# Another written order for the 700 pieces of a kernel's first phase

## The chip, the cores and the metric

The kernel runs on one core of one Trainium2 chip. The metric is the device time of one execution in microseconds. The kernel before took 900.28 us, the median of three runs (898.86, 900.65, 900.28).

## What is computed

Eight batches of 8 heads, 576 tokens, 64 channels. Attention has two parts that are added: one over queries, keys and values averaged in groups of four tokens and repeated four times, and one over a band of 7 tokens. The 4608 x 512 result goes through two weight matrices with a gate between them.

```python
q_d, k_d, v_d = (a.reshape(B, H, S // 4, 4, D).mean(axis=3) for a in (q, k, v))
out_up = np.repeat(sm_attn(q_d, k_d, v_d), 4, axis=2)
scores = np.where(np.abs(pos[:, None] - pos[None, :]) < 4, scale * q @ k.T, -1e9)
out_local = softmax(scores) @ v
x = (out_up + out_local)            # as 4608 x 512
h = x @ w_in                        # 512 x 2048
g = np.where(h >= 1, h, np.where(h <= -1, 0.0, (h + 1) ** 2 / 4))
out = g @ w_out                     # 2048 x 512
```

## The kernel before

Two heads make a pair; 32 pairs, four for each batch. Tokens go through the weight matrices in chunks: one of 512, eight of 384, and two of 512 at the end. The hidden 2048 columns are 16 blocks, f = 0 to 15. Each operand of a large product is split into two words, a high one and the difference to it (`xh`/`xl`, the two halves of a weight block, `gh`/`gl`), and each product takes three matmuls, here called a triple: high by high, high by low, low by high.

The kernel has a first phase, up to the end of the first chunk, and a second phase with a loop over the other chunks. The second phase is not changed. In it the scheduler of the framework places the instructions. The first phase is written as a table, `ORDER`: 700 words that stand for pieces of work. Each piece issues the instructions of one function, in the order of the table, and each engine (TensorE is PE, VectorE is DVE, ScalarE is ACT, GpSimd is POOL, and SP issues the loads) runs its own in that order and waits at the head of its queue. What stands ahead of the table (identity, band, casts of both) is set among the first pieces by the scheduler.

The words: `4.sl@hi1` is pair 4's local scores into the PSUM pool hi1. `lq`, `lk`, `lv`, `lp` load; `qd` and `kd` sum groups of four tokens; `sl` and `sp` are scores, local and pooled; `mx`, `ms`, `ex`, `su`, `nl` and `mp`, `mq`, `e0` to `e2`, `np` are the parts of the two softmaxes; `tl` and `tp` transpose, `al` and `ap` copy that out of PSUM; `pl` and `pp` are the products with the values; `xd`, `x`, `xh`, `xl` write the pair's part of x in two words. `8.lq` to `8.lp` load for pair 8, which belongs to the second phase. `i3.ld` loads block 3 of w_in (512 KB) and `o3.ld` of w_out, `c1` to `c6` unpack it: c1 and c2 on ACT (c2 of odd w_out blocks on DVE), c3 and c4 on DVE, c5 on ACT, c6 on POOL, which writes the low half. `f2.s0` to `f2.s3` are the four triples of the first product for block 2, `u1`, `sq`, `u2`, `gh`, `gl` its gate (DVE, ACT, DVE, ACT, POOL), `m2.0` to `m2.3` its triples of the second product into the four output banks o0 to o3. `f16.s0` to `f16.s3` are already block 0 of the second chunk.

Lines of note: L311 is the band matmul of the local scores, whose left operand is `ident_r` (cast on ACT in L178); L323 the local scores; L377 the pooled scores; L803 is c1, L812 c2, L816 c3, L819 c4, L822 c5 and L826 c6; L847 is a triple's matmul of the first product and L902 of the second; L884 is gl; L910 copies a bank of results and L912 stores it; L643 is the first matmul of pair 8 in the second phase, in the function `join`.

Of the kernel before, what the change touches and what calls it, by code (L numbers as in the profile page):

```python
# [89 lines left out]


ORDER = """
    0.lq 0.z 0.lk 1.lq 1.z 1.lk 0.qd 2.lq 2.z 0.kd 0.sl@hi1 0.sp@hi0 2.lk 1.qd 0.mx 0.mp 0.ms 3.lq
# [4 lines left out]
    1.al i0.c3 i1.ld 0.tp 3.ep 0.vd 2.mq 3.rc 2.e1 1.pp@lo0 3.np 2.e2 3.nl 2.e0 o1.ld 0.ap 2.ep
    3.tl@hi1 2.rc o0.c1 2.nl 3.vs@lo1 3.al o0.c3 3.tp o0.c2 2.np 4.lq 2.tl@hi1 i1.c1 o0.c4 2.vs@hi0
    2.al i2.ld i1.c3 1.pl i1.c2 2.tp o1.c1 i1.c4 0.pp@hi1 1.xh o2.ld o1.c3 2.vd 4.qd 2.ap 1.xl 0.pl  # L100
    1.yh 3.ap o1.c2 2.pp@hi0 i3.ld 3.vd 1.yl 0.xh o1.c4 i2.c1 0.xl 3.pp@lo1 0.yh i2.c3 i0.c2 4.lv
    0.yl o1.c5 i0.c4 4.sl@hi1 o2.c1 o1.c6 o3.ld i2.c2 3.pl 4.mx 2.pl i0.c5 i2.c4 3.xh 4.ms i0.c6
    4.lp 2.xh 3.yh 3.xl i2.c5 4.sp@hi1 i4.ld 2.yh 2.xl f0.s0 4.ex i2.c6 3.yl 4.mp f0.s1 o0.c5 2.yl
    i3.c1 4.su f0.s2 o0.c6 o4.ld i1.c5 f0.s3 4.mq 4.vd o3.c1 i1.c6 4.e1 f0.u1 4.e0 5.lq o2.c3 f1.s0
    4.e2 i3.c3 f0.sq f1.s1 4.ep o3.c3 5.lk o2.c2 f0.u2 f1.s2 i3.c2 4.rc f1.s3 o2.c4 i5.ld f0.gh
    f2.s0 4.nl i4.c1 f0.gl f2.s1 f1.u1 o4.c1 f2.s2 5.qd o5.ld o2.c5 f2.s3 i3.c4 f1.sq m0.0 4.np
    o2.c6 i3.c5 f1.u2 m0.1 i6.ld f2.u1 f1.gh i3.c6 4.tp@hi1 5.kd i5.c1 m0.2 o3.c2 4.ap f1.gl m0.3
    f2.sq o6.ld f3.s0 o5.c1 f2.u2 4.tl@hi1 i5.c3 f2.gh f3.s1 o3.c4 4.al f3.s2 5.lp i4.c3 i5.c2
    o4.c3 f3.s3 o5.c3 o3.c5 i7.ld 4.pl@hi1 i5.c4 i4.c2 4.pp o5.c2 o3.c6 i6.c1 m1.0 4.xd o4.c2 m1.1
    5.lv i4.c4 o6.c1 4.x f2.gl m1.2 i4.c5 5.vd i8.ld m1.3 4.xh 5.sl@hi1 i4.c6 i5.c5 f3.u1 i7.c1  # L110
    m2.0 5.mx i5.c6 6.lk m2.1 f3.sq 5.ms f4.s0 4.xl 6.lq f3.u2 5.ex f4.s1 f3.gh f4.s2 i9.ld i6.c3
    i8.c1 f4.s3 o4.c4 i6.c2 m2.2 o6.c3 f4.u1 i7.c3 o4.c5 f5.s0 o8.ld f4.sq i6.c4 o6.c2 f5.s1 f4.u2
    o5.c4 i6.c5 m2.3 o6.c4 i7.c2 5.sp@hi1 f4.gh o4.c6 o7.ld f5.s2 f5.s3 f5.u1 o6.c5 5.su f5.sq
    f3.gl i6.c6 o5.c5 6.qd i9.c1 f5.u2 i10.ld o6.c6 o8.c1 f6.s0 6.kd f6.s1 5.mp f6.s2 o9.ld 5.mq
    o7.c1 f6.s3 f4.gl m3.0 5.e0 f6.u1 5.e2 m3.1 i7.c4 5.e1 6.lp m3.2 i8.c3 i10.c1 5.ep o5.c6 m3.3
    5.rc o10.ld i7.c5 5.nl m4.0 f6.sq 5.np i7.c6 f5.gh m4.1 f6.u2 o9.c1 m4.2 i11.ld o7.c3 i8.c2
    m4.3 o8.c3 o7.c2 f5.gl f7.s0 o8.c2 f7.s1 f6.gh o11.ld i10.c3 f7.s2 o10.c1 o7.c4 f7.s3 i10.c2
    i9.c3 5.tp@hi1 o8.c4 i9.c2 i12.ld 5.ap i10.c4 m5.0 o8.c5 i9.c4 m5.1 i8.c4 i10.c5 m5.2 f6.gl
    i9.c5 o13.ld m5.3 i8.c5 5.tl@hi1 f7.u1 o11.c1 i9.c6 m6.0 f7.sq m6.1 o12.ld o7.c5 o10.c3 m6.2
    i12.c1 f7.u2 i8.c6 m6.3 5.al f9.s0 o9.c3 f7.gh i13.ld i12.c3 o10.c2 f8.s0 o9.c2 o7.c6 f8.s1  # L120
    i11.c1 f8.s2 i12.c2 o10.c4 i15.ld f8.s3 o13.c1 o9.c4 5.pl@hi1 i11.c3 o12.c1 5.pp 5.xd 5.x f8.u1
    o8.c6 o10.c5 6.lv 6.vd f9.s1 o9.c5 f7.gl f9.s2 f8.sq i14.ld i11.c2 f9.s3 f8.u2 i10.c6 6.sl@hi1
    5.xh f9.u1 i13.c1 m7.0 o13.c3 7.lp f9.sq 6.mx o10.c6 m7.1 i15.c1 o13.c2 m7.2 7.lq 6.ms o9.c6
    f8.gh m7.3 f9.u2 7.lk 6.ex f10.s0 5.xl i14.c1 6.sp@hi1 o14.ld f10.s1 f9.gh 6.mp f8.gl f10.s2
    6.su f10.s3 7.qd f9.gl o15.ld m8.0 6.mq f10.u1 6.e1 m8.1 6.e0 7.kd m8.2 f10.sq i11.c4 6.e2 m9.0
    i12.c4 i11.c5 m9.1 6.ep f10.u2 o14.c1 i11.c6 m9.2 6.rc i12.c5 6.nl m8.3 f10.gh i12.c6 6.np
    f11.s0 o15.c1 f11.s1 o11.c3 f12.s0 o13.c4 f11.s2 o11.c2 f10.gl o13.c5 f11.s3 o12.c3 f12.s1
    o11.c4 o12.c2 m10.0 f11.u1 o13.c6 o11.c5 6.tp@hi1 f11.sq f12.s2 i13.c3 6.ap f12.s3 f11.u2
    o11.c6 i13.c2 m9.3 f11.gh o12.c4 6.tl@hi1 f12.u1 f11.gl m10.1 o12.c5 6.al m10.2 f12.sq i14.c3
    m10.3 i13.c4 i14.c2 6.pl@hi1 f12.u2 o12.c6 i13.c5 6.pp 7.lv 7.vd 8.lp f12.gh m11.0 i13.c6 6.xd  # L130
    m11.1 6.x m11.2 i14.c4 6.xh m11.3 o14.c3 i14.c5 i15.c3 7.sl@hi1 8.lq 8.lk o14.c2 o15.c3 f12.gl
    i15.c2 o15.c2 f13.s0 7.mx f13.s1 i14.c6 7.ms m12.0 m12.1 7.ex i15.c4 f14.s0 o14.c4 i15.c5
    f14.s1 o15.c4 o14.c5 f13.s2 6.xl o15.c5 f13.s3 m12.2 f13.u1 i15.c6 7.sp@hi1 f13.sq f14.s2 7.mp
# [1125 lines left out]
```

## Time and profile before

| | |
|---|---|
| median of the runs | 900.28 us |
| profiled execution, first to last instruction | 900.0 us |
| PE busy | 885.3 us |
| DVE, ACT, POOL busy | 563.7, 467.9, 375.0 us |
| first phase (to the last triple of f16) | 155.85 us |
| mean granted TensorE clock | 0.997 |

The profiled execution's own time stands in the profile only as this span; it is 0.3 us below the median of the runs. A busy PE is not PE at its peak, since matmuls overlap: the pitch from one start to the next says more than the duration. PE's clock has two levels, 1.2 and 2.4 GHz; a granted clock of 1.0 is the upper one.

### The profile page before, as it was taken

What the parts mean: (1) busy time and instruction counts of PE and PEld (TensorE: products, weight loads), DVE (VectorE), ACT (ScalarE), POOL (GpSimd) and SP (SyncE); (2) the same over time, 40 slices, a digit from 0 to 9 for tenths busy, and PEclk for the clock granted to TensorE, in tenths of its full rate; (3) what the DMA queues carried; (4) which work ended last, traced back from release to release, by engine and by line L of the source; (5) the groups of instructions that cost most, each with busy time, mean ns of one, the idle gap of its engine ahead of it and who ended that gap; (6) DMA issues with size and microseconds to landing.
All of it is one profiled execution on the core that took longest, in us unless ns stands there. A gap on an engine that the chain in (4) does not pass through costs nothing.

```text
span 900.0 us, 19773 instructions
## 1 busy us (share of the span) xinstructions
PE 885.3 (98%) x7808; PEld 798.0 (89%) x7808; DVE 563.7 (63%) x1077; ACT 467.9 (52%) x1025; POOL 375.0 (42%) x361
## 2 busy tenths in 40 slices
...
GB/s 344 120 213 319 126 57 53 97 110 128 90 115 115 91 106 116 122 120 116 113 103 89 101 133 103 105 139 92 91 127 106 83 51 83 122 109 141 105 126 53
DMA packets 67884, 106.47 MB, mean 118 GB/s; under 512 B 5808, under 2 KB 33456, under 8 KB 67792
## 3 DMA queue, kind: packets, MB, share of 16 engines
...
q8 instruction: 61, 1.00, 0.4%
...
q10 hardware_dynamic: 144, 0.05, 0.0%
...
## 4 chain that ended last, share of the span: by engine, by line
PE 84%; DVE 7%; ACT 4%; issue 3%; POOL 2%; DMA 0%; SPq 0%; DVEq 0%; ACTq 0%; POOLq 0%
PE ffn_o L902 37%; PE ffn_h L847 28%; PE ffn_h L1015 7%; PE score_ps L643 2%; PE turn_ps L771 1%; PE value_ps L667 1%; DVE m L819 1%; PE local_ps L768 1%; PE value_ps L625 1%; DVE m L816 1%; DVE u L869 1%; DVE u L875 1%; POOL gl L884 1%; ACT u L872 1%; DVE sums L924 1%
## 5 line engine op out<-in xcount | busy, mean ns | idle before, releaser
L884 POOL TENSOR_TENSOR gl<-u,gh 128x384 fp32r<-128x384 f32 (+1 forms) x176 | 197.0, 1120 | 400.4 <-ACT gh L881 320.3
L902 PE MATMUL ffn_o<-w_o,gh 128*128 128x512 f32 x1152 | 347.5, 383 | 0.0
L847 PE MATMUL ffn_h<-xh,w_i 128*128 128x384 f32 (+1 forms) x1184 | 301.2, 336 | 2.5 <-POOL w_i L826 2.1
L902 PEld LDWEIGHTS ffn_o<-w_o,gh 128*128 128x128 f32 x1152 | 212.0, 190 | 25.2 <-issue 0.6
L847 PEld LDWEIGHTS ffn_h<-xh,w_i 128*128 128x128 f32 x1184 | 209.5, 189 | 16.9 <-POOL w_i L826 2.9
L902 PE MATMUL ffn_o<-w_o,gl 128*128 128x512 f32 x576 | 218.9, 380 | 0.4 <-POOL gl L884 0.4
L847 PE MATMUL ffn_h<-xl,w_i 128*128 128x384 f32 (+1 forms) x592 | 197.3, 333 | 0.0
L872 ACT ACTIVATE u<-u 128x384 f32<-128x384 f32 (+1 forms) x176 | 97.4, 553 | 133.5 <-DVE u L869 133.5
L881 ACT CAST gh<-u 128x384 fp32r<-128x384 f32 (+1 forms) x176 | 95.3, 542 | 118.8 <-DVE u L875 117.3
L869 DVE TENSOR_SCALAR u<-m 128x384 f32<-128x384 f32 (+1 forms) x160 | 76.1, 476 | 127.3 <-ACT m L868 126.9
L875 DVE SCALAR_TENSOR_TENSOR u<-m,u 128x384 f32<-128x384 f32 (+1 forms) x160 | 103.2, 645 | 78.0 <-ACT u L872 78.0
L902 PEld LDWEIGHTS ffn_o<-w_o,gl 128*128 128x128 f32 x576 | 109.3, 190 | 16.4 <-POOL gl L884 0.8
L847 PEld LDWEIGHTS ffn_h<-xl,w_i 128*128 128x128 f32 x592 | 111.9, 189 | 2.2
L868 ACT COPY m<-ffn_h 128x384 f32<-128x384 f32 (+1 forms) x132 | 63.8, 484 | 51.1 <-PE ffn_h L847 42.4
L720 ACT ACTIVATE sl<-sl 128x640 f32<-128x640 f32 x24 | 17.7, 739 | 55.1 <-POOL sl L694 55.1
L581 POOL TENSOR_TENSOR xl<-x,xh 128x576 fp32r<-128x576 f32 (+4 forms) x32 | 35.3, 1110 | 16.6 <-ACT xh L580 16.6
L826 POOL TENSOR_TENSOR w_o<-m,w_o 128x512 fp32r<-128x512 f32 x16 | 24.1, 1517 | 31.2 <-ACT w_o L822 31.2
L924 DVE SCALAR_TENSOR_TENSOR sums<-sums 128x128 f32<-128x128 f32 (+1 forms) x72 | 33.0, 459 | 1.6
L694 POOL TENSOR_TENSOR sl<-sl,mxl 128x640 f32<-128x640 f32 x24 | 30.2, 1260 | 2.3 <-DVE mxl L693 1.7
L924 DVE SCALAR_TENSOR_TENSOR words<-sums,words 128x512 fp32r<-128x512 f32 x16 | 17.7, 1109 | 17.7 <-ACT words L928 17.7
L826 POOL TENSOR_TENSOR w_i<-m,w_i 128x512 fp32r<-128x512 f32 x16 | 22.6, 1415 | 11.6 <-ACT w_i L822 11.4
L1041 POOL TENSOR_TENSOR m<-both 128x256 f32<-128x256 f32 x14 | 10.7, 765 | 39.0 <-DVE both L1040 33.8
(179 smaller groups left out, 1183.4 us busy)
## 6 DMA issues: line engine op xcount, KB each, us to landing
...
```

The source lines that it names most:

```text
L581: nc.gpsimd.tensor_tensor(xl[:, p, dst], x[:, part], xh[:, p, dst], op=ALU.subtract)
L826: nc.gpsimd.tensor_tensor(w[:, 1], raw[name, f, "m"], w[:, 0], op=ALU.subtract)
L847: ins = nc.tensor.matmul(htiles[c, f], wi[:, wt, cc * P : (cc + 1) * P], turns(xt[:, cc, ts]), start=(cc == 0 and xt is xh and wt == 0), s ...
L868: utiles["copied"] = nc.scalar.copy(m, h)
L869: nc.vector.tensor_scalar(utiles[c, f], m if c > 0 else h, -1.0, 1.0, op0=ALU.max, op1=ALU.add)
L872: nc.scalar.activation(u, u, AF.Square, scale=0.5)
L875: utiles["last"] = nc.vector.scalar_tensor_tensor(u, utiles["m"] if c > 0 else h, 1.0, u, op0=ALU.max, op1=ALU.min)
L881: nc.scalar.copy(gh, utiles[c, f])
L884: nc.gpsimd.tensor_tensor(gl, utiles.pop((c, f)), gh, op=ALU.subtract)
L902: ins = nc.tensor.matmul(o, gt[:, ts], turns(weights["o", f][:, wt, :]), start=f == 0 and n == 0, stop=f == NFC - 1 and n == 2,)
L924: return nc.vector.scalar_tensor_tensor(out, a, 1.0, b, op0=ALU.mult, op1=op)
L1015: ins = nc.tensor.matmul(ps, left(wt, k), right(xt, k), start=not more and k == 0 and wt == xt, stop=k == 1 and xt == 1, skip_group_check= ...
```

## The change

The table is replaced by another with 704 words. They are the same pieces, and four new ones, `r.0` to `r.3`: the copy of an output bank and its store, which `m15.0` to `m15.3` did before as their last act. Loads, unpacking, attention and products all stand in another order; the second product takes the four banks in another order from block to block. Three functions now make their PSUM tile whichever piece of the two that share it comes first, and three calls of `keep_up` (extra matmuls, of which both tables ask for none) are gone.

```diff
 ORDER = """
-    0.lq 0.z 0.lk 1.lq 1.z 1.lk 0.qd 2.lq 2.z 0.kd 0.sl@hi1 0.sp@hi0 2.lk 1.qd 0.mx 0.mp 0.ms 3.lq
...
-    8.lv 7.pp m13.3 7.xd 7.x m15.0 m15.1 7.xh m14.3 7.xl m15.2 m15.3 f16.s3
+    0.lq 0.lk 0.z 1.lq 0.sl@hi1 1.lk 0.qd 0.kd i1.ld i1.c1 0.sp@hi0 0.mx 0.mp o3.ld 2.lq 0.mq 2.lk
...
+    f13.gl f15.s2 f14.s3 7.e2 f12.gl f15.s3 7.ep 7.rc o13.c5 7.nl f14.u1 o14.c6 7.np f15.u1 f14.sq
+    m12.2 o15.c5 o13.c6 f15.sq m12.0 f14.u2 m11.1 f14.gh m12.1 f16.s0 f15.u2 m13.2 7.tp@hi1 6.xl
+    m13.0 m12.3 m13.3 o15.c6 7.ap f15.gh f14.gl f15.gl 7.tl@hi1 m14.0 7.vd m15.0 7.al f16.s1
+    7.pl@hi1 7.pp@hi1 7.xd m13.1 m14.3 m14.1 7.x f16.s2 m14.2 7.xh 7.xl m15.3 m15.1 m15.2 r.0 r.1
+    8.lv r.2 8.lk f16.s3 r.3 8.lp
 """.split()
...
         def vs(pool, tag, spare=0):
-            ps = t["tp_ps"] = pool.tile([P, 2, 512], F32, name="tp_ps", tag=tag)
-            keep_up(ps[:, 1, 384:], spare)
+            if "tp_ps" not in t:
+                t["tp_ps"] = pool.tile([P, 2, 512], F32, name="tp_ps", tag=tag)
+            ps = t["tp_ps"]
...
         elif piece == 2:
             raw["low", name, f] = t[:, :, 0]
-            if (name, f, "m") in raw and (name, f) not in ON_VECTOR:
+            if (name, f) not in ON_VECTOR:
                 raw["low", name, f] = t.rearrange("p n t -> p (n t)")[:, 0:512]
...
-        if f == NFC - 1:
-            osb = temp("osb")
-            nc.scalar.copy(osb, o)
-            rows = out[CHUNKS[c][0] : CHUNKS[c][0] + CHUNKS[c][1], :].rearrange("(a b) d -> b a d", a=2)
-            nc.sync.dma_start(rows[t * P // 2 : (t + 1) * P // 2], osb)
+        if f == NFC - 1 and c > 0:
+            result(c, t)
+
+    def result(c, t):
+
+        osb = temp("osb")
+        nc.scalar.copy(osb, places["o"](t))
+        rows = out[CHUNKS[c][0] : CHUNKS[c][0] + CHUNKS[c][1], :].rearrange("(a b) d -> b a d", a=2)
+        nc.sync.dma_start(rows[t * P // 2 : (t + 1) * P // 2], osb)
...
+            elif kind == "r":
+                result(0, int(what))
```

The first place is ACT's queue at the very start. Before, from the load of `members` on:

```order
L239 DMA own_2_87<-members 128x360
L180 ACT_TABLE_LOAD
L180 CAST band_r<-band_sb 128x64
L178 CAST ident_r<-ident 128x128
L394 ACTIVATE sp,sums<-sp_ps,mxp 128x144 x2
L363 ACTIVATE sl<-sl_ps 128x640
```

And now, the same stretch:

```order
L240 DMA own_2_87<-members 128x360
L181 ACT_TABLE_LOAD
L181 CAST band_r<-band_sb 128x64
L803 ACTIVATE raw_i_150<-raw_i_150 128x512
L179 CAST ident_r<-ident 128x128
L395 ACTIVATE sp,sums<-sp_ps,mxp 128x144
L812 ACTIVATE raw_i_150<-raw_i_150 128x512
```

The first piece of block 1 of w_in (L803) has come between the two casts, though the cast of `ident_r` stands ahead of the table in the code.

The second place is PE's queue between pair 6's local scores (`sl_ps`) and its pooled scores (`sp_ps`); `ffn_o` are triples of the second product, `ffn_h` of the first. Before:

```order
L323 MATMUL sl_ps<-k_sb,q_sb 64x64 x20
L902 MATMUL ffn_o_706<-w_o_1262,gh 128x512 x2
L902 MATMUL ffn_o_706<-w_o_1262,gl 128x512
L902 MATMUL ffn_o_710<-w_o_1262,gh 128x512 x2
L902 MATMUL ffn_o_710<-w_o_1262,gl 128x512
L902 MATMUL ffn_o_711<-w_o_1262,gh 128x512 x2
L902 MATMUL ffn_o_711<-w_o_1262,gl 128x512
L902 MATMUL ffn_o_719<-w_o_1262,gh 128x512 x2
L902 MATMUL ffn_o_719<-w_o_1262,gl 128x512
L847 MATMUL ffn_h_702<-xh,w_i_1228 128x512 x2
L847 MATMUL ffn_h_702<-xl,w_i_1228 128x512
L377 MATMUL sp_ps<-kd,first_qd 64x144 x6
```

And now:

```order
L324 MATMUL sl_ps<-k_sb,q_sb 64x64 x20
L847 MATMUL ffn_h_728<-xh,w_i_1356 128x512 x2
L847 MATMUL ffn_h_728<-xl,w_i_1356 128x512
L902 MATMUL ffn_o_732<-w_o_1295,gh 128x512 x2
L902 MATMUL ffn_o_732<-w_o_1295,gl 128x512
L847 MATMUL ffn_h_728<-xh,w_i_1356 128x512 x2
L847 MATMUL ffn_h_728<-xl,w_i_1356 128x512
L378 MATMUL sp_ps<-kd,first_qd 64x144 x6
```

Five triples stood between them, and three stand there now; for pair 4 it is the other way, eight triples where its neighbours' local values stood.

The third place is SP's queue at the end of the phase, around the four stores of results (`out`). Before, from pair 8's loads of q and k on:

```order
L201 DMA q_sb<-qT 128x576
L201 DMA k_sb<-kT 128x576
L210 DMA v<-vw 128x640
L912 DMA out<-osb 64x2x512 x4
L201 DMA q_sb<-qT 128x576
```

And now:

```order
L202 DMA q_sb<-qT 128x576
L916 DMA out<-osb 64x2x512 x2
L211 DMA v<-vw 128x640
L916 DMA out<-osb 64x2x512
L202 DMA k_sb<-kT 128x576
L916 DMA out<-osb 64x2x512
```

The load of k for pair 8 stood ahead of all four stores and stands behind the third now.

## Rows read from the trace of the kernel before

**Rows 1.** Windows: length; busy PE, PEld, DVE, ACT, POOL; clock; DMA share; GB/s.
```profile
104.00:106.00 2.00, 2.00 (x7) 1.55 (x6) 2.00 (x4) 2.00 (x5) 1.42 (x1) 0.50 0.58 156
...
44.28:155.85 111.57, 105.72 (x796) 88.07 (x795) 97.99 (x147) 84.72 (x155) 72.67 (x49) 0.98 0.44 153
...
155.85:900.00 744.15, 739.60 (x6362) 680.08 (x6361) 437.84 (x874) 357.38 (x803) 291.73 (x286) 1.00 0.33 106
```

**Rows 2.** Waits of PE, 0 to 160 us: us in total, times, longest.
```profile
PE sl_ps L311 <- DVE x L541: 2.3, 1, 2.3
...
PE ffn_h L847 <- POOL w_i L826: 2.1, 2, 1.8
...
PE sp_ps L377 <- DVE sl L353: 1.9, 2, 1.2
...
PE tp_ps L431 <- ACT own L482: 1.1, 1, 1.1
...
PE ffn_o L902 <- POOL gl L884: 0.4, 1, 0.4
...
PE sl_ps L342 <- DVE mxl L334: 0.4, 1, 0.4
...
PE ffn_h L847 <- DVE u L875: 0.3, 1, 0.3
```

**Rows 3.** Timeline of PE around its longest wait: start, us, work [idle before].
```profile
101.88 0.55 PE L311 MATMUL sl_ps<-band_r,ident_r 128*128 128x384 f32 x2 [2.26 <-DVE x L541]
...
103.21 1.22 PE L902 MATMUL ffn_o<-w_o,gh 128*128 128x512 f32 x2
...
107.57 0.59 PE L847 MATMUL ffn_h<-xh,w_i 128*128 128x512 f32 x2
...
109.13 0.71 PE L377 MATMUL sp_ps<-kd,first_qd 64*64 64x144 f32 x12 [0.75 <-DVE sl L353]
...
113.11 0.59 PE L902 MATMUL ffn_o<-w_o,gh 128*128 128x512 f32 x2
...
113.76 0.59 PE L902 MATMUL ffn_o<-w_o,gh 128*128 128x512 f32 x2
```

**Rows 4.** Timeline of ACT at the start.
```profile
2.72 0.29 ACT L178 CAST ident_r<-ident 128x128 fp32r<-128x128 f32 x1
```

**Rows 5.** Timeline of PE at the start.
```profile
5.20 0.53 PE L311 MATMUL sl_ps<-band_r,ident_r 128*128 128x384 f32 x2
...
6.01 0.92 PE L323 MATMUL sl_ps<-first_k,first_q 64*64 64x64 f32 x40 [0.29 <-DMA first_k<-kT]
```

**Rows 6.** Windows of the first loads, and DVE's first work on a load.
```profile
1.00:3.80 2.80, 2.75 (x13) 2.75 (x14) 0.35 (x1) 1.73 (x3) 0.77 (x5) 1.00 0.63 143
...
1.00:7.80 6.80, 5.93 (x74) 5.27 (x74) 2.69 (x5) 1.73 (x3) 1.80 (x7) 1.00 0.83 262
...
4.83 0.75 DVE L291 TENSOR_REDUCE first_q<-first_q 128x144 f32<-128x576 f32 x1 [1.75 <-DMA first_q<-qT]
```

**Rows 7.** Lines, 0 to 160 us, ACT: busy us, mean ns.
```profile
L803 ACT ACTIVATE raw_i<-raw_i 128x512 f32<-128x512 f32 x16 | 13.2, 826 | 0.0
```

**Rows 8.** The phase's end: ACT's result copies, PE, k_sb's loads.
```profile
L910 ACT COPY osb<-ffn_o 128x512 f32<-128x512 f32 x4 | 2.3, 586 | 1.5 <-PE ffn_o L902 1.2
...
155.36 0.49 PE L847 MATMUL ffn_h<-xh,w_i 128*128 128x384 f32 x2
...
157.99 0.81 PE L643 MATMUL score_ps<-k_sb,q_sb 64*64 64x64 f32 x40
...
DMA to landing us min/median/max: 2.8/3.3/7.9
```

**Rows 9.** GpSimd's weight differences and gl: ns min/median/max, first and last start.
```profile
L826 POOL TENSOR_TENSOR w_o<-m,w_o x16: 1270/1474/1977, 38.7 to 138.9; 128x512 fp32r<-128x512 f32 x16
...
L884 POOL TENSOR_TENSOR gl<-u,gh x17: 1001/1297/3888, 50.9 to 158.9; 128x512 fp32r<-128x512 f32 x16, 128x384 fp32r<-128x384 f32 x1
```

**Rows 10.** DVE's shift of a weight block: ns min/median/max.
```profile
L816 DVE TENSOR_SCALAR m<-raw_i x16: 405/508/1610, 22.3 to 131.0; 128x512 int32<-128x512 int32 x16
```

More of the change, by code (lines that the diff above doesn't have):

```diff
@@ L98 @@
[L98 to L133, printed above, removed]
@@ L134 @@
-    o14.c6 f14.s3 f13.u2 m12.3 7.su f13.gh o15.c6 f15.s0 7.mq f14.u1 7.e1 f15.s1 7.e2 f13.gl f14.sq
-    f15.s2 7.e0 f15.s3 f14.u2 7.ep m13.0 f14.gh 7.rc f15.u1 f16.s0 f14.gl 7.nl f15.sq f16.s1 f16.s2
-    7.np m13.1 f15.u2 7.tp@hi1 f15.gh m14.0 f15.gl 7.ap m13.2 7.tl@hi1 m14.1 7.al m14.2 7.pl@hi1
-    8.lv 7.pp m13.3 7.xd 7.x m15.0 m15.1 7.xh m14.3 7.xl m15.2 m15.3 f16.s3
+    0.lq 0.lk 0.z 1.lq 0.sl@hi1 1.lk 0.qd 0.kd i1.ld i1.c1 0.sp@hi0 0.mx 0.mp o3.ld 2.lq 0.mq 2.lk
+    1.z 1.kd 3.lq i1.c3 1.sl@lo1 1.qd 0.e1 1.mx i1.c2 0.ms 1.sp@lo0 3.lk i3.ld 1.mp 3.kd 1.ms 0.ex
@@ new lines @@
+    0.su 2.sl@hi1 0.e2 3.z 4.lq 0.e0 1.ex 1.lv 1.mq 1.e1 0.ep 1.su 2.kd 2.mx i2.ld 1.e0 0.rc
+    3.sl@lo1 o2.ld 3.qd 2.lv 2.z o3.c1 i3.c1 3.lv 3.mx 2.ms 0.nl 0.np 3.ms 2.ex 3.sp@hi1 1.e2 3.mp
+    0.tl@hi0 3.ex 1.vs@lo1 i2.c1 1.ep 0.al 3.mq 2.qd 1.rc 3.e2 1.np 1.vd 0.lv 3.su 1.nl 3.e0
+    1.tp@lo1 2.sp@hi0 3.e1 o1.ld 3.ep 1.ap 2.mp 2.su 2.mq i0.ld 1.tl@lo0 o2.c1 o0.ld 1.al o3.c2 2.e0
+    o1.c1 o2.c3 0.tp@lo1 0.vs@lo1 0.ap i0.c1 3.rc 0.vd 2.e2 i3.c3 3.nl 1.pp@lo0 2.e1 3.np i2.c3
+    3.tl@hi1 3.al 3.tp@lo1 1.pl@lo0 3.vs@lo1 i1.c4 4.lk i0.c3 4.kd i1.c5 4.lp 2.ep i2.c2 3.ap 2.rc
@@ new lines @@
+    2.nl 2.tl@hi1 o13.ld i0.c2 2.np 2.tp@hi0 2.al o0.c1 i2.c4 o3.c3 o3.c4 2.vs@hi0 1.xh 2.vd o0.c3
+    o5.ld 1.yh 2.ap o1.c3 o2.c2 i0.c4 i4.ld i3.c2 i6.ld 0.pp@hi1 i4.c1 i1.c6 3.vd 1.yl 0.pl@hi1
+    o1.c2 4.qd 0.yh 1.xl 2.pp@hi0 i5.ld 4.vd o0.c2 o1.c4 i4.c3 2.pl@hi0 i3.c4 o0.c4 o13.c1 0.xh
+    i0.c5 i15.ld o2.c4 i0.c6 o4.ld 3.pp@lo1 i4.c2 i2.c5 2.xh i7.ld 0.yl 0.xl i5.c1 i4.c4 o14.ld
+    3.pl@lo1 2.xl 2.yh 3.xh 2.yl 4.sl@hi1 5.lk f0.s0 i3.c5 4.mx f0.s1 o15.ld 3.xl o2.c5 i4.c5 4.ms
+    o0.c5 f0.s2 i7.c1 i2.c6 i12.ld f0.s3 i3.c6 o0.c6 i5.c3 o2.c6 f1.s0 f0.u1 4.lv f1.s1 f0.sq f0.u2
@@ new lines @@
+    o8.ld f1.s2 f1.s3 4.sp@hi1 f2.s0 i5.c2 o3.c5 f1.u1 i7.c3 i9.ld f2.s1 3.yh i10.ld o6.ld f0.gh
+    o1.c5 f2.s2 f0.gl o7.ld 3.yl 4.mp 4.mq m0.2 f1.sq i5.c4 f1.u2 4.ex m0.3 5.lq 4.su 4.e0 5.kd 4.e1
+    o1.c6 4.e2 4.ep f2.s3 o9.ld f1.gh 4.rc f3.s0 m0.1 f2.u1 i7.c2 f1.gl i8.ld i6.c1 f2.sq i5.c5
+    i4.c6 f3.s1 f3.s2 4.nl i6.c3 o3.c6 i9.c1 o5.c1 4.np i6.c2 m0.0 f2.u2 m1.1 i7.c4 4.tp@hi1 f3.s3
+    4.ap f4.s0 o6.c1 f3.u1 f3.sq i14.ld o4.c1 f4.s1 i6.c4 4.tl@hi1 i11.ld m1.3 o5.c2 i9.c3 i6.c5
+    5.lp f3.u2 m1.0 f4.s2 f4.s3 f3.gh o11.ld 4.al i5.c6 o9.c2 m1.2 5.qd 4.pp@hi1 o7.c1 o4.c3 i6.c6
@@ new lines @@
+    f2.gh 4.xd o5.c3 4.pl@hi1 i8.c1 o4.c2 i13.ld f2.gl f5.s0 f4.u1 4.x f5.s1 m2.2 i10.c1 o6.c3 f5.s2
+    i7.c5 o5.c4 o11.c2 o4.c4 m2.0 5.sl@hi1 i9.c2 f4.sq f4.u2 f5.s3 5.mx i7.c6 o7.c2 o6.c2 m2.1 f3.gl
+    4.xh f6.s0 o5.c5 f5.u1 m2.3 i12.c1 6.lq 5.ms o5.c6 i8.c3 o8.c1 m3.2 f6.s1 5.sp@hi1 o13.c2 f5.sq
+    o10.ld o6.c4 f5.u2 o4.c5 m3.1 5.lv f6.s2 f4.gh f4.gl 5.ex f7.s0 6.lk i8.c2 5.mp o4.c6 6.qd 5.mq
+    5.e1 5.su f7.s1 5.e0 o6.c5 i15.c1 i8.c4 f6.s3 5.e2 m3.0 f6.u1 i11.c1 f7.s2 o6.c6 m3.3 i10.c3
@@ new lines @@
+    f7.s3 5.ep m4.0 m4.3 i9.c4 5.rc f5.gh o15.c2 5.np f6.sq i8.c5 f6.u2 f5.gl o14.c1 o10.c1 o9.c1
+    i12.c3 m4.1 m5.3 m5.1 i8.c6 5.nl f6.gh m4.2 4.xl f7.u1 f8.s0 5.vd f6.gl 5.tp@hi1 f7.sq i11.c3
+    f8.s1 5.ap f8.s2 6.kd i9.c5 m5.0 m5.2 m6.0 f7.u2 i13.c1 m6.3 5.tl@hi1 o7.c3 o9.c3 i11.c2 o7.c4
+    i9.c6 m6.2 f8.s3 o9.c4 m6.1 o7.c5 o10.c3 i12.c2 f9.s0 f9.s1 o12.ld f7.gh 5.al 5.pp@hi1 f9.s2
+    o7.c6 i10.c2 o10.c2 o8.c3 5.pl@hi1 5.xd o8.c2 f7.gl f8.u1 i10.c4 f9.s3 i10.c5 m7.2 i11.c4 m7.3
+    o8.c4 f8.sq 6.lp i11.c5 i10.c6 o9.c5 m7.1 f8.u2 i12.c4 5.x i12.c5 f10.s0 f10.s1 i14.c1 6.sl@hi1
@@ new lines @@
+    f10.s2 i13.c3 i11.c6 o15.c1 6.lv f9.u1 o8.c5 i12.c6 6.mx f9.sq m7.0 f8.gh o9.c6 o11.c1 f10.s3
+    6.ms o8.c6 6.ex f9.u2 6.sp@hi1 f11.s0 f8.gl 6.mp 6.mq f11.s1 f10.u1 f9.gh 6.e0 6.e1 m8.1 f9.gl
+    m8.0 6.su f10.sq f10.u2 6.e2 o10.c4 m8.2 m9.0 i15.c3 7.lq o14.c3 i13.c2 6.ep 5.xh f11.s2 f11.s3
+    o10.c5 6.rc m8.3 7.lk o12.c1 6.np m9.2 f10.gh f12.s0 5.xl f12.s1 o10.c6 f10.gl 6.nl i15.c2
+    o12.c3 6.tp@hi1 m9.1 m10.2 7.qd 6.ap f11.u1 f11.sq i13.c4 o12.c2 i15.c4 o11.c3 m9.3 i13.c5
+    o11.c4 f12.s2 i13.c6 6.vd o14.c2 6.tl@hi1 6.al o11.c5 m10.3 f12.s3 o14.c4 6.pp@hi1 i14.c3
```

13 lines of the change are left out of this document (5 added, 8 removed).

## The prediction

> **What bounds the kernel now.** I read the page first: TensorE is busy nearly all of the span, so what counts is where it is not. The windows view, cut where the phases part, shows that: after 155.85 us PE is busy 739.6 of 744.15 us, and the code there is unchanged; in the first phase up to there it is idle in places [rows 1]. The phase's end moves the end of the kernel one for one, as PE stands in one queue and waits for almost nothing later. Third, the waits of PE inside the phase: seven entries, 2.3 + 2.1 + 1.9 + 1.1 + 0.4 + 0.4 + 0.3 = 8.5 us [rows 2]. Fourth, the timeline around the largest: PE stood 2.26 us until 101.88, and from 103.21 to 107.57 four triples of matmuls took 4.36 us where a triple at the granted clock of 1.0 takes 0.65 (113.11 to 113.76), 2.6 for four [rows 3]. The clock was granted at 0.50 there [rows 1], the 1.2 GHz level; after the waits of 1.1 and 1.8 us [rows 2] it was not lowered. So that wait cost 1.8 us more. Whatever order is chosen, it cannot win more than 8.5 + 1.8 = 10.3 us, about 1.1% of the span.
>
> **Removed.** I credit all 10.3 us at first, and then charge what stays or comes anew. For three of the causes the new order clearly helps: pair 4's pooled scores stand behind eight triples (5.2 us) instead of behind its local values, against a wait of 1.2 us; the last pieces of a w_i are written earlier ahead of the product that needs them (counted in the two tables at 0.65 a triple, 4.3 us of PE work stand between them on average over 16, from 1.9); and pair 6's scores stand 4.0 us of PE work behind pair 5's values, before 1.9, against the wait of 2.26 us.
>
> **Added at the start.** ScalarE now has the first piece of w_in block 1 between the casts of band_r and ident_r, and PE's first real matmul needs ident_r. Before, ident_r was cast at 2.72 us [rows 4], PE came to the band matmul at 5.20, right behind its warm-up, and to the scores at 6.01 [rows 5]. Now ident_r waits for a load: the fifth on SP after band, behind two q and two k. Through it, 32 + 45 + 4 x 288 + 512 KB = 1.78 MB must have moved. In the trace of before 262 GB/s over 6.8 us is 1.78 MB by 7.8 us; the first q (0.37 MB) had moved by 3.7 (143 GB/s over 2.8 us is 0.40 by 3.8), and VectorE took it at 4.83, 1.1 later [rows 6]. So the block lands at 8.9. Then 0.83 for its activation [rows 7] and 0.29 for the cast: 10.05; the band matmuls take 0.53 and the scores begin at 10.6 instead of 6.01: **+4.6 us** (4.2 to 5.0, by half a microsecond of landing). Queued behind the waiting ScalarE instruction stand the cast and all exponentials; DVE's first maximum waits for PE. Nothing covers this: PE has no other work that can run.
> The Trainium skill ("DMA: Bandwidth & Descriptors", Anatomy of one DMA) gives a DMA a fixed 2.0 us and 436 GB/s; were this load issued at 3 us, five issues into SP's queue, and alone, it would land at 6.2 by that estimate, and the term would be 1.9 us. The rows say otherwise, since four loads lie ahead of it and 1.78 MB were through only at 7.8 us.
> PE then idles from the end of its warm-up to 10.05, about 5 us, more than twice the idle time that was followed by the 0.50 clock. I take the same cost, **+1.8 us**; the ends are nothing (PE waits for other engines in that stretch anyhow) and 3.6 (twice as long).
>
> **Added at the end.** The load of pair 8's k is now issued after the third result. That result copies bank o2 after the last matmul ahead of f16.s3. Call T the start of f16.s3 (155.36 before). The copy runs T+0.2 to T+0.8 (0.59, [rows 8]); SP issues the result, then k at about T+1.2. k_sb lands 2.8 at the least and 3.3 us in the median after its issue, so at T+4.0 to T+4.5. PE wants it at T+2.63 (157.99 before). Before, k stood on SP ahead of all four results. **+1.9 us** (1.4 to 2.6, the pooled scores need k's sums from DVE too). The copies of the four results themselves cost nothing: same four, on ScalarE, which waits for PE there.
>
> **What stays.** Four places, each from rows. (1) The 1.1 us at the first transposes: one more 0.65 us piece now covers it, 0.5 stays. (2) Pair 6's pooled scores stand behind three triples (1.9 us), before behind five. DVE needs two operations and what is queued ahead; before, it was through only 5.8 us after the last score matmuls were started (103.3 to 109.1, [rows 3]). So 0 to 3.8; I take 2.0. (3) At the end GpSimd has, from f12.gl to f14.gl, three weight differences at 1.47, the xl of pair 6, taken as long as a gl, and a gl at 1.30 [rows 9], 7.0 us, where PE has eight triples at 0.65, one of f16 at 0.49 and two sets of transposes, taken as 1.0, 6.7; then f15.gl at 1.30 against one triple. 0.3 + 0.65, so 1.0. (4) gl stands closer ahead of its product (1.4 us of PE work on average, from 2.3): 0.7, from nothing to 3. Together **+4.2 us**; the ends are 1 (only the places where GpSimd or PE are short by count) and 9 (as many waits as before, somewhere else).
> The rest of the diff is neutral: `keep_up` is called with zero everywhere in both tables, and the third piece of every block that is split on ScalarE precedes its second in both, so the changed condition picks the same words.
>
> **Sum.** 4.6 + 1.8 + 1.9 + 4.2 - 10.3 = +2.2 us on the profiled 900.0, 902.2. The median of the runs is 0.3 above the profile: 902.5.
>
> **Rivals.**
> *Faster, the early conversions.* By the time of f0.s0 the new table has nine blocks through both of their DVE steps, before five. Those steps are quick while GpSimd is quiet and slow beside it: the shift takes 0.41 at the least and 1.61 at the most [rows 10], and the longest wait of PE was for a DVE sum that stood behind such steps. If they leave the DVE queue short, the waits of pair 6 and of gl vanish; what stays is 1.0, and if the stretch after the start costs 0.6 at the lower clock because PE waits for DVE there anyway, 4.6 + 0.6 + 1.9 + 1.0 - 10.3 = -2.2: 898.1. With k landing at its minimum it is 897.6. It decides from residual waits below 1.4, where the sum passes -1.8. For it: DVE is 98.0 us busy in 111.6 [rows 1]. Against: DVE and ScalarE also start 4 to 5 us later, and their early idle time is what the conversions need.
> The Trainium skill ("GPSIMD Engine Reference", Key points) has GpSimd contend with VectorE for SBUF interfaces; by it the four shifts moved ahead cost 4 x 0.41 instead of as much as 4 x 1.61 us of DVE, up to 4.8 less. The durations agree [rows 10]; whether the path is shorter by that no row shows.
> *No change.* The residual waits are 2.0 (pair 6 does not wait, GpSimd keeps up): 900.3. For it: both the start and the end loss are sure, and together with the gain they cancel but for this.
> *Much slower.* DVE begins 4.5 us later, becomes the bound of the later part, and there are as many waits as before, 8.5 instead of 4.2: 906.8. A second idle time over 2 us, at k, could bring the low clock back, 1.8 more. Against: it would need most gains to fail.
> *The start loss does not come*, because the load lands before PE's warm-up ends: -4.2 in all, 896.1. It would need 1.78 MB by 4 us; I give this under 0.03, inside the faster case.
>
> **How the numbers follow.** Forecast 0.36, much slower 0.12, no change 0.32, faster 0.20. What a measurement can tell from no change is about 0.2%, 1.8 us: under 898.5 is faster, over 902.1 slower. The forecast's own range (901.3 to 904.5) reaches a little under that border, and the no-change case a little over it, so these even out: faster 0.20, same 0.33, slower 0.47. The range that holds 8 in 10 takes most of the faster case and of the much slower one: 898.0 to 906.5. The bounds of all terms at once would be 896.6 to 910.2; that they fall together is unlikely.
>
> **What would show it.** Right: PE idle from about 5 to about 10 us, waiting on ScalarE; ident_r cast behind raw_i's activation at 9 to 10 us; a clock of 0.50 after it; a wait of PE for k_sb at the first score_ps of 1.4 us or more; no wait on w_i. Wrong: ident_r before 5 us; k_sb landed when PE comes to the first join; the first score_ps before 157 us, or after 163. If the sum fails, I expect it in the residual waits, the least certain term.

## The result, and the profile after

The kernel after takes 905.07 us (median of 904.08 to 906.49); before, run beside it, 899.57 us. The ratio on record is 1.0077, 95% interval 1.006 to 1.0094 (these two medians of four runs alone give 1.0061): slower, as forecast. The time is 2.6 us above the forecast of 902.5, over the forecast's own range of 901.3 to 904.5 and inside the wide one of 898.0 to 906.5. The profiled execution of the kernel after took 905.15 us with a span of 903.4, 3.4 more than the profiled span of before; the medians stand 5.5 apart. That gap is a finding of its own (below).

The waits of PE in the first phase of the kernel after, to be held against [rows 2]: what was waited for, us in total, times, longest.
```profile
PE sl_ps L312 <- ACT ident_r L179: 4.9, 1, 4.9
PE score_ps L643 <- issue: 4.1, 1, 4.1
...
PE tp_ps L470 <- ACT own L445: 0.5, 1, 0.5
PE pl_ps L503 <- ACT xd L537: 0.4, 1, 0.4
PE ffn_h L847 <- DVE u L875: 0.2, 1, 0.2
```
Of the seven entries, 8.5 us in sum, only the last is left, with 0.2 us. Two small waits at other lines came in: the transposes of pooled scores (L470) and local values (L503) wait 0.5 and 0.4 us for ScalarE. Together 0.5 + 0.4 + 0.2 = 1.1 us. (The 1.1 us before the warm-up, the same in both kernels, are left out.) Two large ones stand above them, 4.9 and 4.1 us, at the phase's two ends.

The start, which answers to [rows 4, 5, 7]. ScalarE's timeline (start, us, work, idle time before and what ended it), then PE's:
```profile
9.07 0.66 ACT L803 ACTIVATE raw_i<-raw_i 128x512 f32<-128x512 f32 x1 [6.08 <-DMA raw_i<-w_in]
9.64 0.28 ACT L179 CAST ident_r<-ident 128x128 fp32r<-128x128 f32 x1
```
```profile
1.05 4.02 PE L1069 MATMUL warm<-xl 128*128 128x128 f32 x20 [1.05 <-DVE xl L173]
9.97 0.90 PE L312 MATMUL sl_ps<-band_r,ident_r 128*128 128x384 f32 x2 [4.91 <-ACT ident_r L179]
10.80 1.44 PE L324 MATMUL sl_ps<-first_k,first_q 64*64 64x64 f32 x38
```
ident_r is cast at 9.64, no longer at 2.72, since the activation ahead of it in ScalarE's queue stood 6.08 us for its load. PE was through with its warm-up at 5.07 and could not begin until 9.97.

The end, which answers to [rows 8]. SyncE's issues (start, us); PE's last matmuls of the phase and its first of pair 8; two transfers of the window from 153 us (KB, us to landing):
```profile
149.54 3.35 SPq L916 DMA_DIRECT2D out<-osb  x2
152.98 0.54 SPq L211 DMA_DIRECT2D v<-vw  x1
153.57 0.54 SPq L916 DMA_DIRECT2D out<-osb  x1
154.21 0.54 SPq L202 DMA_DIRECT2D k_sb<-kT  x1
```
```profile
152.18 0.49 PE L847 MATMUL ffn_h<-xh,w_i 128*128 128x384 f32 x2
...
154.46 0.33 PE L847 MATMUL ffn_h<-xl,w_i 128*128 128x384 f32 x1
158.89 1.35 PE L643 MATMUL score_ps<-k_sb,q_sb 64*64 64x64 f32 x40 [4.11 <-issue]
```
```profile
v<-vw SPq DMA_DIRECT2D x1, 320.0 KB, 3.4
k_sb<-kT SPq DMA_DIRECT2D x1, 288.0 KB, 4.6
```
PE is out of work at 154.79 (154.46 + 0.33). k is issued at 154.21 and lands 4.6 us later, at 158.8; the scores begin at 158.89. The trace calls that wait "issue", and in runs below it names an operation of ScalarE; the landing ends later than either. What was late is found only by laying the landing beside the first matmul.

The stretches of lowered clock, which answer to [rows 1]. Windows: length; busy PE, PEld, DVE, ACT, POOL; granted clock; DMA share; GB/s.
```profile
7.67:14.50 6.83, 4.53 (x72) 3.47 (x76) 1.94 (x4) 1.08 (x3) 3.11 (x6) 0.50 1.03 403
48.06:157.50 109.44, 106.18 (x822) 89.36 (x818) 87.31 (x141) 81.97 (x154) 68.70 (x50) 1.00 0.37 126
158.89:164.69 5.80, 5.80 (x63) 5.42 (x64) 3.18 (x6) 0.07 (x1) 3.14 (x3) 0.50 0.46 139
```
The clock is 0.50 (1.2 GHz) from 7.67 to 14.50, and in the second stretch until 164.69. Both times it fell while PE stood idle in the long wait, the second time between 157.5 and 158.0 us (0.86 on the mean there). From f0.s0 to 157.5 us it is not lowered, and the wait for x that ended at 101.88 in before [rows 3] has no counterpart.

### The profile page after: what moved, and what is told of

Its sections match the earlier page's. It is cut to its first block, busy times and chain, and to the rows that moved or that the text cites. A ratio compares the mean times of both kernels' runs of the same rounds, so it can differ in the third digit from the quotient of the medians.

```text
span 903.4 us, 19755 instructions
## 1 busy us (share of the span) xinstructions
PE 887.6 (98%) x7808; PEld 801.3 (89%) x7808; DVE 555.7 (62%) x1077; ACT 466.6 (52%) x1025; POOL 372.9 (41%) x361
## 4 chain that ended last, share of the span: by engine, by line
PE 91%; DVE 3%; ACT 2%; DMA 1%; issue 1%; SPq 0%; POOL 0%; ACTq 0%; DVEq 0%
PE ffn_o L902 39%; PE ffn_h L847 31%; PE ffn_h L1019 7%; PE score_ps L643 2%; PE turn_ps L771 1%; PE value_ps L667 1%; PE pl_ps L526 1%; DVE sums L928 1%; PE local_ps L768 1%; PE value_ps L625 1%; PE sl_ps L324 1%; DVE u L875 1%; PE pl_ps L503 1%; DMA raw_i<-w_in 1%; PE score_ps L611 1%
## 5 line engine op out<-in xcount | busy, mean ns | idle before, releaser
L884 POOL TENSOR_TENSOR gl<-u,gh 128x384 fp32r<-128x384 f32 (+1 forms) x176 | 194.7, 1107 | 401.0 <-ACT gh L881 324.7
L1038 DVE TENSOR_TENSOR both<-ffn_h,both 128x256 f32<-128x256 f32 x14 | 5.9, 424 | 32.8 <-PE ffn_h L1019 31.8
```

Of the source, the lines that this page charges most:

```text
L884: nc.gpsimd.tensor_tensor(gl, utiles.pop((c, f)), gh, op=ALU.subtract)
```

## The experiments

Each ran beside the kernel before, and a ratio is always to it. Its median was 897.7 to 898.3 us in these series, so one thousandth is 0.9 us. "Under the kernel after" is against 905.12 us, its median in the first experiment; ident_r first, k early, both, the results last and k late ran in other series than that.

**The kernel after, once more, for the same comparison.**

> The kernel after once more, unchanged, for a median and a profile on the same chip as the others. Theory A: both waits of 4 to 5 us and both stretches of half clock are there again in the profile, and the ratio to before is again 1.006 to 1.009. A rival on the earlier profile (its stretches of half clock were chance): one of them is missing, and the ratio nearer to 1.003.

Measured: 905.12 us, 1.0078 (1.0062 to 1.0094), span 902.0. Both waits are there again, 4.0 and 4.0 us. The loss is no accident of one series: 7.4 us against the 897.74 of before beside it. Of the clock only the second stretch is there as expected. At the start (window as above, then PE's first band matmuls):
```profile
7.67:14.50 6.83, 4.86 (x97) 3.88 (x97) 1.95 (x4) 1.42 (x5) 2.86 (x7) 1.00 1.03 405
```
```profile
9.64 0.90 PE L312 MATMUL sl_ps<-band_r,ident_r 128*128 128x384 f32 x2 [3.95 <-ACT ident_r L179]
```
The row says 1.00, but the scores behind these two matmuls start 0.83 us after them (10.47), as in the first profile at 0.50 (9.97 and 10.80). This trace holds no record of the clock before 13.3 us, and the view prints 1.00 where there is none. The 20 matmuls of the warm-up took 4.64 us here and 4.02 there. So PE ran slowly behind the wait both times, but only the first profile shows the clock falling in it.

**ident_r first.** In the table:
```diff
-    ... 0.kd i1.ld i1.c1 0.sp@hi0 ... 3.lq i1.c3 1.sl@lo1 1.qd 0.e1 1.mx i1.c2 ...
+    ... 0.kd i1.ld 0.sp@hi0 ... 3.lq 1.sl@lo1 1.qd 0.e1 1.mx i1.c1 i1.c3 i1.c2 ...
```


> The kernel after, with the conversion of w_in's piece i1.c1 (and the shift i1.c3 that needs it) written behind 1.mx, so that on ScalarE the cast of ident_r stands ahead of the activation that waits for raw_i1. Theory A (two places alone lose the time): PE's wait of 4.9 us at L312 goes, the scores of pair 0 start at about 6.0 us instead of 10.8, the stretch of 0.50 clock from 7.7 to 14.5 us goes with it (2.2 us more), and since nothing else bounds the first phase, f0.s0 starts 5 to 7 us earlier (41 to 43 us instead of 48.06) and the time falls by as much, from 905.1 to 898 to 900 us. Rival B (VectorE takes the gain back): VectorE is busy for some 90% of the phase, so what PE wins at the start it loses in new waits for VectorE before 155 us: f0.s0 early, but the third result no earlier than about 150 us, and the time falls by less than 2.5 us, to 902.6 or above.

Measured: 899.05 us, 1.0012 (1.0001 to 1.0023), 6.1 us under the kernel after. ScalarE's timeline at the start:
```profile
2.93 0.29 ACT L179 CAST ident_r<-ident 128x128 fp32r<-128x128 f32 x1
...
9.22 0.69 ACT L803 ACTIVATE raw_i<-raw_i 128x512 f32<-128x512 f32 x1
```
ident_r is cast at 2.93 and raw_i's activation stands behind the first exponentials. The scores of pair 0 begin at 6.14, f0.s0 at 42.14 instead of 48.06 (5.9 earlier), the last triple of results at 146.06 instead of 151.97 (5.9 earlier). What is won at the start arrives at the end of the phase whole; rival B, that VectorE would take it back, is out. The wait at the scores of pair 8 stays (4.0 us).

**k early.**
```diff
-    7.lp f12.u2 8.lq m11.0 ...
+    7.lp f12.u2 8.lq 8.lk m11.0 ...
-    8.lv r.2 8.lk f16.s3 r.3 8.lp
+    8.lv r.2 f16.s3 r.3 8.lp
```


> The kernel after, with pair 8's k load written directly behind its q load instead of behind the third remaining result. Theory A: PE's wait of 4.1 us at L643 (score_ps) and the 0.50 clock from 157.9 to 164.7 us go, some 2.7 us more, and nothing else is late there: the time falls by 5.5 to 7 us, to 898 to 899.6 us. Rival C (the stores are what is late, not k's place): with k there early the first matmul of pair 8 waits for something else, v or the stores of the results, for 1.5 us or more, and the time falls by under 4 us, to 901 or above.

Measured: 899.77 us, 1.0017 (1.0007 to 1.0026), 5.4 us under the kernel after, just short of the 5.5 to 7 expected. The first matmuls of pair 8 carry no idle time in PE's timeline now: the last result triple starts its last matmul at 152.44 and pair 8 at 155.19, 2.75 us later; in the kernel after these were 6.92 us apart. Nothing else was late behind k, so rival C in its first form is out.

**Both.**

> The kernel after with both edits: i1.c1 and i1.c3 behind 1.mx, and pair 8's k load behind its q load. Theory A: the two losses are separate, so the sum of both gains, some 10.5 to 14 us against the kernel after: 891 to 894.6 us, which is 5 to 8.5 us under the kernel before. Rival B: what is won at the start is taken back by waits for VectorE, so that this is as fast as the edit at the end alone, within 2 us: 896.5 to 899.6 us.

Measured: 893.73 us, 0.9951 (0.9936 to 0.9967), span 891.5: 11.4 us under the kernel after, where the two edits alone gave 6.1 and 5.4, together 11.5. The losses are separate and add up, and this version is faster than both kernels. All its waits of PE in the first phase:
```profile
PE tp_ps L470 <- ACT own L445: 0.5, 1, 0.5
PE ffn_h L847 <- DVE u L875: 0.4, 2, 0.3
PE pl_ps L503 <- ACT xd L537: 0.4, 1, 0.4
PE ffn_h L847 <- ACT m L868: 0.3, 1, 0.3
```
The wait before the warm-up left out, 0.5 + 0.4 + 0.4 + 0.3 = 1.6 us. This is the new order without its two faults, and so the worth of the order itself: 4.2 us by the medians (893.73 against 897.94).

**The start's clock alone.** The warm-up made longer, so that PE works until shortly before ident_r is there (until 8.93 us, as it turned out):
```diff
-WARM = 10
+WARM = 22
```


> The kernel after with 22 in place of 10 of the warming multiplications at the start (same length each, about 0.40 us, so TensorE works until about 9.9 us, just before ident_r is there). The wait for ident_r stays, only TensorE's idleness before it is filled. Theory A (the start's loss has two terms, the wait and the half clock that follows it): the scores of pair 0 still start at about 10.8 us, but the 0.50 clock from 7.7 to 14.5 us doesn't come, and the time falls by what the low clock alone costs, the 4.5 us of work from 9.97 us on at half speed, so 1.5 to 2.5 us under the kernel after. Rival D (the work behind the idle stretch is held by loads and VectorE, so its clock is worth nothing): within 0.7 us of the kernel after.

Measured: 901.85 us, 1.0049 (1.003 to 1.0068), 3.3 under the kernel after in the same series, more than the 1.5 to 2.5 expected. The first band matmuls and the window after the start (columns as above); then the 5.80 us from the first scores of pair 8 on, here and in the kernel after of the same series:
```profile
9.78 0.56 PE L312 MATMUL sl_ps<-band_r,ident_r 128*128 128x384 f32 x2 [0.85 <-ACT ident_r L179]
```
```profile
9.90:14.00 4.10, 4.10 (x100) 3.07 (x100) 2.62 (x5) 1.03 (x3) 0.77 (x3) 1.00 1.03 409
```
```profile
156.39:162.19 5.80, 5.80 (x68) 5.31 (x69) 3.19 (x7) 0.92 (x3) 3.40 (x4) 0.71 0.52 161
```
```profile
158.00:163.80 5.80, 5.80 (x64) 5.42 (x65) 3.18 (x6) 0.17 (x1) 3.15 (x3) 0.53 0.46 137
```
The clock is 1.00 behind the wait at the start, and f0.s0 comes at 45.92, against 47.39 in the kernel after of the same series: 1.5 us is what the slow stretch cost there. (From the first band matmul to f0.s0 it is 36.14 us here, 37.75 in that run and 38.09 in the first profile, so 1.6 and 1.9.) Another 1.6 of the 3.2 us between the two spans (902.0, 898.8) come after the scores of pair 8 began, 742.4 us against 744.0, where less of the time was at half clock: 0.71 on the mean of the first 5.80 us, not 0.53. This edit doesn't touch that place. So rival D is out, the sum was right only at the start, and the price of half clock behind one and the same wait (3.9 here, 4.0 there) differs from one execution to another.

**v behind k.**
```diff
-    8.lv r.2 8.lk f16.s3 r.3 8.lp
+    r.2 8.lk 8.lv f16.s3 r.3 8.lp
```


> The kernel after with pair 8's v load written behind its k load, so that k is issued about 1.1 us earlier (153.1 instead of 154.21 us) and no load stands in front of it, but still behind the third result. Theory A (k's place decides, and 3.4 us to landing, as with k late in the kernel before, is its own length): k lands at about 156.5 instead of 158.8 us, the wait at L643 falls from 4.1 to 1.5 to 2 us, and as after that kernel's wait of 1.6 us no half clock follows: 4 to 5.3 us under the kernel after. Rival E (the landing of 4.6 us comes from the four stores and vq, not from v): k lands 4.4 us or more after its issue, the wait is 2.8 us or more, the half clock stays, and the gain is 0.8 to 1.5 us.

Measured: 901.81 us, 1.0044 (1.0029 to 1.0059), 3.3 us under the kernel after. SyncE's issues, the transfer of k, the first matmuls of pair 8 and the clock behind them:
```profile
153.56 0.55 SPq L202 DMA_DIRECT2D k_sb<-kT  x1
154.21 0.39 SPq L211 DMA_DIRECT2D v<-vw  x1
```
```profile
DMA to landing us min/median/max: 3.1/3.1/3.1
```
```profile
156.80 1.01 PE L643 MATMUL score_ps<-k_sb,q_sb 64*64 64x64 f32 x36 [2.09 <-ACT m L868]
```
```profile
157.00:160.00 3.00, 3.00 (x55) 2.43 (x49) 2.57 (x5) 1.03 (x2) 1.00 (x1) 0.52 0.96 284
```
k lands 3.1 us after its issue instead of 4.6, so v in front of it cost 1.5 us of landing, and 0.65 us of issue (153.56 against 154.21). The wait falls from 4.1 to 2.1. Rival E is out. Theory A was right on k's landing (156.7), nearly on the wait (1.5 to 2 expected) and wrong on the clock: half clock came after 2.1 us too. From the scores of pair 8 to the end it is 743.1 us, against 742.0 with both edits and 744.5 in the kernel after. The gain was 3.3 us and not 4 to 5.3.

**The results written last.**
```diff
-    ... m15.2 r.0 r.1
-    8.lv r.2 8.lk f16.s3 r.3 8.lp
+    ... m15.2
+    8.lv 8.lk f16.s3 r.0 r.1 r.2 r.3 8.lp
```


> The kernel after with its second part undone: the four pieces r.0 to r.3 stand together behind f16.s3 again, after pair 8's k load, so that SyncE issues k ahead of all four stores; the copies on ScalarE and all else keep their order. Theory A: k is issued at about 149 to 150 us, lands 3.3 to 4.6 us later, before TensorE gets to it at 154.8; no wait at L643 and no half clock there: 5 to 6 us under the kernel after, like the edit that writes k behind q. Rival G (issuing the stores later holds the second phase up, by the buffers of the results): the first multiplications of the second phase's results wait, and the gain is under 3 us.

Measured: 899.07 us, 1.0006 (0.999 to 1.0021), 6.1 us under the kernel after (905.12 in another series). SyncE's issues:
```profile
146.72 0.33 SPq L211 DMA_DIRECT2D v<-vw  x1
147.14 0.38 SPq L202 DMA_DIRECT2D k_sb<-kT  x1
149.71 4.66 SPq L916 DMA_DIRECT2D out<-osb  x4
```
k goes out at 147.14, earlier than expected, since only v, whose buffer was free by 146.72, stands in front of it. The four stores start where two of them started before (149.71 against 149.54). No wait at pair 8, and the second phase isn't held up (742.2 us from the scores of pair 8 to the end, 742.0 with both edits): rival G is out. So writing the results early brought nothing that these runs can tell (899.07 here, 899.77 with k early); what the pieces of their own did was to let a load be written behind three stores that wait.

**k late, in the kernel before.**
```diff
-    ... 7.sl@hi1 8.lq 8.lk o14.c2 ...
+    ... 7.sl@hi1 8.lq o14.c2 ...
-    ... 7.xl m15.2 m15.3 f16.s3
+    ... 7.xl m15.2 8.lk m15.3 f16.s3
```


> The kernel before with one piece moved: pair 8's k load written behind m15.2, at the end of the phase, as the new order has it. Theory A: the end's loss comes alone: PE waits 3 to 5 us at L643 and the 0.50 clock follows for about 6.8 us (2.7 us more): slower by 5 to 7.5 us, 904.6 to 907 us. Rival C (k's place costs little, the slow landing came from the stores and v queued ahead of it in the new order): k lands 3.3 us or less after its issue, the wait is under 2 us, no low clock follows, and the kernel is slower by under 2 us, 899.6 to 901.6 us.

Measured: 899.21 us, 1.0009 (0.9996 to 1.0022). SyncE's issues and pair 8's first matmuls:
```profile
153.19 0.58 SPq L201 DMA_DIRECT2D k_sb<-kT  x1
```
```profile
156.69 0.81 PE L643 MATMUL score_ps<-k_sb,q_sb 64*64 64x64 f32 x40 [1.61 <-ACT m L868]
```
A miss for theory A, which had 5 to 7.5 us: PE waited 1.6 us, and no half clock followed. With no v load in front and the stores closer together k was issued 1.03 us after the last result triple began (153.19, 152.16), where in the kernel after it was 2.24 (154.21, 151.97), and landed 3.4 us later. k behind three closely issued stores costs a wait of 1.6 us here, and by the medians 1.3 us, which the interval doesn't tell from nothing; behind waiting stores and v, and with the clock, it costs five to six. Rival C holds for this kernel in kind (it had 3.3 us or less to landing, and 899.6 us at the least), and v's part is shown above.

**The kernel before, once more.** Why do profiles and medians differ?

> The kernel before once more, unchanged. The two profiled spans stand 3.4 us apart and the medians 5.5, so one of the two profiles is not typical. Theory F: it is that of before, whose wait of 2.3 us for the x of pair 2 at 104 us and the half clock behind it come in some executions only (with k late in the same kernel that wait was 0.9 us and no half clock came): the wait is about 0.9 us this time, no half clock in the first phase, and the profiled span is about 897 us, 2 to 3 us under the earlier 900.0. Rival: the wait of 2.3 us and the half clock at 104 us are there again, span 899.5 to 900.5, and the difference lies in the profile of after.

Measured: 897.93 us median, 1.0006 (0.9993 to 1.002), but the profiled execution took 900.19, span 898.4. Its longest wait, and the clock where it was 0.50 in [rows 1]:
```profile
PE sl_ps L311 <- DVE x L541: 2.3, 1, 2.3
```
```profile
104.00:106.00 2.00, 2.00 (x11) 1.76 (x10) 2.00 (x4) 2.00 (x5) 1.23 (x1) 1.00 0.39 84
```
Theory F was half right: the half clock is gone, the wait is not. (The 0.9 us that it took from the run with k late was a wait at 64.70 us, for another pair.) It took an execution at the median to see more:

> The kernel before once more, for a profile of an execution at its median (about 897.7 us; the two profiled ones took 900.2 and more). Theory F': no half clock in the first phase, the wait for the x of pair 2 is about 0.9 us instead of 2.3 (as in the run with k late), TensorE's waits up to 155 us sum to 5.5 to 6.5 us instead of 8.5, and the scores of pair 8 start at 154.3 to 155.3 us instead of 158.0. Rival: the waits sum to 8 us or more again, and what the median runs save lies in the second phase, behind 155 us.

Measured: 898.04 us, 0.9996 (0.9978 to 1.0013); the profiled execution took 897.96, span 896.1. Its waits, beside [rows 2]:
```profile
PE sp_ps L377 <- DVE sl L353: 2.2, 2, 1.2
PE ffn_h L847 <- POOL w_i L826: 2.0, 2, 1.7
PE tp_ps L431 <- ACT own L482: 1.1, 1, 1.1
...
PE sl_ps L342 <- DVE mxl L334: 0.4, 1, 0.4
PE ffn_h L847 <- DVE u L875: 0.3, 1, 0.3
PE sl_ps L311 <- DVE x L541: 0.3, 1, 0.3
```
These make 6.3 us, and the wait for x is 0.3 instead of 2.3. The three profiles of before fit together within half a microsecond: 6.3 us of waits and span 896.1; 9.0 us and 898.4; 8.5 us with 1.8 of half clock and 900.0. The prediction's profile was of an execution that was 3.9 us longer than one at the median, 3.8 of it at that one wait and the clock behind it.

What made x late is in VectorE's queue. From the timeline of all engines, GpSimd's differences, two of VectorE's steps ahead of x, and x, in the profile that the prediction used; then the same in the execution at the median:
```profile
92.85 3.12 POOL L826 TENSOR_TENSOR w_o<-m,w_o 128x512 fp32r<-128x512 f32 x2
...
93.19 1.61 DVE L816 TENSOR_SCALAR m<-raw_i 128x512 int32<-128x512 int32 x1
...
96.20 1.78 DVE L819 CUSTOM_DVE_ANT_0 m<-m,raw_o 128x1024 uint16<-128x1024 uint16 x1
...
101.08 0.74 DVE L541 TENSOR_TENSOR x<-pl_ps,xd 128x576 f32<-128x576 f32 x1
```
```profile
93.45 4.21 POOL L826 TENSOR_TENSOR w_o<-m,w_o 128x512 fp32r<-128x512 f32 x2
...
93.81 0.54 DVE L816 TENSOR_SCALAR m<-raw_i 128x512 int32<-128x512 int32 x1
...
95.45 1.06 DVE L819 CUSTOM_DVE_ANT_0 m<-m,raw_o 128x1024 uint16<-128x1024 uint16 x1 [0.64 <-ACT raw_o L812]
...
99.67 0.75 DVE L541 TENSOR_TENSOR x<-pl_ps,xd 128x576 f32<-128x576 f32 x1
```
The shift of raw_i took 1.61 us in the one and 0.54 in the other, the later step 1.78 and 1.06; x started at 101.08 and at 99.67. In the second, GpSimd's pair of differences took 4.21 us where it took 3.12. The other two traces of this order fall in with these: in the second profile of before the three times are 1.62, 1.78 and 3.10 us and the wait is 2.3, and with k late they are 0.54, 0.99 and 4.19 and PE does not wait there. The same instructions in the same order took VectorE's time in the one execution and GpSimd's in the other, and a wait is 2.3 us or 0.3. Four traces agree on this; no run changes it on purpose.

## Why the prediction came out as it did

The forecast's class was right and its number 2.6 us low. Of its five terms two were right; the other three were mis-sized, partly against each other, so that the number is in part luck.

- **The start, +4.6.** Right. ident_r was cast at 9.64 (forecast 9.76), the scores began at 10.80 (10.6). Against the same order with ident_r first it is 4.7 us (6.14), and 4.2 against the one with both edits (6.56). The load had landed by 9.07, when ScalarE began on it; 8.9 was forecast.
- **The half clock behind it, +1.8.** Right: 1.5 to 1.9 by the warm-up experiment. Both together 5.7 by f0.s0 (48.06 against 42.34), where 6.4 had been forecast, and 6.1 by the medians.
- **The end, +1.9.** The term that failed most: 4.1 us of wait, and 2.5 us more behind it (from the scores of pair 8 to the end of the span 744.5 us, with both edits 742.0), 6.6 by the profiles, 5.4 by the medians. The step "SP issues the result, then k at about T+1.2" failed first: with T = 152.18 it was T+2.03, since v's issue stood ahead of the third result, which the prediction did not list among what k is queued behind. The step "2.8 at the least and 3.3 us in the median" failed next: it was 4.6 with v's 320 KB on the way, and 3.1 when v stood behind. And half clock after this wait was left out of the sum and stood only in a rival. The forecast expected its error in the residual waits; the larger one was here.
- **What stays, +4.2.** Far too high: 1.1 us, its lower end. The first transposes wait 0.5, as forecast, though at another line and for another piece of ScalarE's work (L445, not L482). Pair 6's scores, for which 2.0 were charged, and GpSimd's tail and gl, 1.7 together, waited for nothing. That is what the rival of the early conversions said of this term, and VectorE was indeed less busy from f0.s0 on: 87.3 of 109.4 us, before 98.0 of 111.6 [rows 1]. But no run moves the conversions alone, so that they are the cause is not shown. The rival's premise, that the shift is quick while GpSimd is quiet and slow beside it, holds in one execution and not in another (0.54 us beside GpSimd's 4.21).
- **Removed, -10.3.** Right for the execution that was profiled, too high for the kernel: in an execution at the median 6.3 us of waits were there to be removed, and no half clock. "The median of the runs is 0.3 above the profile" set a time beside a span: in the eleven runs with both, the time is 1.75 to 1.86 us above the span, so the profiled execution of before took an estimated 901.8, not 900.0. That is 1.5 above the median it was set beside, and 3.5 or more above the 897.7 to 898.3 of the later series. (The list of waits also has 0.3 for first_k and 0.2 for own, which the sum of 8.5 leaves out.)

Summed with what was measured: 5.7 + 6.6 + 1.1 - 10.3 = +3.1 on the profiled span of 900.0, where the two profiles stand 3.4 apart; and 5.7 + 6.6 + 1.1 - 6.3 = +7.1 on the span of 896.1, where the medians of one series stand 7.4 apart. The forecast of +2.2 was near the first because the missing 4.7 at the end and the 3.1 too much in what stays nearly cancelled. The much slower rival's time, 906.8, was nearer (1.7 us), but its cause, VectorE as the bound with as many waits as before, isn't what happened; of it only the low clock at k came true.

What stays open: how much of the order's worth the early conversions are, why one execution gives VectorE and another GpSimd the shorter time, and why half clock followed a wait of 2.3 us in one execution of before and not in the next.
